# A linear-attention and SwiGLU kernel: o of the shared remainder tile by single heads, behind o of the chunks

## The chip, the core and the metric

The kernel runs on one core of one Trainium2 chip. Its engines work side by side, each in the order of its own queue: TensorE (PE, matrix products, with a queue of weight loads shown as PEld), VectorE (DVE), ScalarE (ACT), GpSimd (POOL), and SyncE (SP), which issues transfers. TensorE writes into PSUM, eight banks of 128 partitions by 512 float32; VectorE and ScalarE read them. The metric is the device time of one execution in microseconds.

## The reference

Linear attention without a softmax, a norm per head, then a gated feed-forward block (FFN) with a norm in front:

```python
# q, k, v: (8 batches, 8 heads, 576 rows, 64), float32
kv = np.einsum('bhsd,bhse->bhde', k, v)
out = np.einsum('bhsd,bhde->bhse', q, kv)                 # "o"
rms = np.sqrt(np.mean(out * out, axis=-1, keepdims=True) + 1e-06)
x = (out / rms * g_norm)                                  # then heads side by side: (4608, 512)
rms = np.sqrt(np.mean(x * x, axis=-1, keepdims=True) + 1e-06)
xn = x / rms * rms_g
g = xn @ w_gate                                           # 512 x 1536
silu = g * (1.0 / (1.0 + np.exp(-g)))
return silu * (xn @ w_val) @ w_out                        # 1536 x 512
```

## The kernel before

**Tiles.** Each batch has 576 rows: 4 chunks of 128 (NC = 4) and a remainder of 64 (REM). The remainders of two batches share a tile of 128 rows. So there are nine groups of 512 rows for the FFN: one per batch from its chunks, and one, group B, from the eight remainders. Heads go in pairs: j = 0 to 3 (NS = 4) numbers the pairs, and of a pair the even head lies on partitions 0 to 63 of `qT` and `kv`, the odd one on 64 to 127.

**The backbone.** The FFN of a group is 24 slots of the first product (12 gate slots and 12 val slots in turn, `mm1`, four matmuls of 128x512 each, L694) and 16 of the second (`mm2`, L729). A gate's result is read by ACT (silu, L703), a val's by DVE (product h, L712). The results of `mm1` lie in turn in the three PSUM banks of the pool mm1; those of `mm2` in the two banks of o2; the attention has the three banks of att. A bank is written again only when its last readers are done.

**Attention beside it.** While group g runs, the attention of the next batch is laid into the slots by a planner (`Placer`). It gives every operation an engine and a cost, puts it into the first slot in which its inputs are there and the engine has room left, and `emit` writes the program out slot by slot: first the slot's operations of ACT, DVE, POOL and SP, then the FFN's own matmuls, then the attention's matmuls. Each engine then works in that order. The costs only decide the order; the chip has its own times. `P.psum` also keeps count of the att banks: its list `P.tiles` has an entry per bank taken, with the operations that must be done before it is free.

**The steps of one batch** (`place_attention`, batches 2 to 7): q is transposed by DMA (`qT_dma`, L342; the remainder's rows L345); kv is computed (`kv_mm`, L281) and copied (`kv_half`, L310); then o of the chunks, `o_heads` (L375): 32 matmuls, each with one head, 64 rows of the array and 128 columns, 64 columns streamed. It writes four banks, two of o2 and two of att; even and odd heads go to different banks. For batch 2 and the odd batches 3, 5 and 7, o of the shared remainder tile follows: `o_rem` (L362), 8 matmuls over all 128 rows of the array and 64 of its columns, a pair of heads at a time (`kvs` holds zeros off its two diagonal blocks), 128 columns streamed, into one att bank. The two halves of the tile take the kv of two batches (`of`).

Of each of the five (or four) tiles, ACT makes a square (`sq_`, L410) and a copy (`outa_`, L414). POOL multiplies the square by the squared norm weights (`wsq`, L465), DVE sums square and product over each head (`red`, L473, twice a tile). A chain of small DVE steps makes the factors of both norms (L512 to L530), DVE scales the copies (`xna_`, L540 and L545), and SP issues transposes into x (`x_dma`, L603). The pool sq has three buffers: the fourth tile's square waits until the first tile's product has been summed.

Beside it, POOL issues the loads of the next batch's k and v (L200, and L196 for remainders) and casts q. During batch 2, ACT and DVE also multiply the weights by the norm gains (`fold`, L850 and L852), and POOL issues the loads of batch 3 at fixed slots (L963 to L965).

Of the kernel before, what the change touches and what calls it, by code (L numbers as in the profile page):

```python
# [10 lines left out]
FP32 = mybir.dt.float32  # L11
BF16 = mybir.dt.bfloat16
# [3 lines left out]
ACT = mybir.ActivationFunctionType  # L16
# [71 lines left out]
def kernel(  # L88
# [12 lines left out]
    nc = tc.nc  # L101
    B, H, S, D = q.shape
# [3 lines left out]
    NC = 4  # L106
# [16 lines left out]
    outa_p = pool("outa", 6)  # L123
    sq_p = pool("sq", 3)
# [7 lines left out]
    mm1_p = pool("mm1", 3, space=bass.MemoryType.PSUM)  # L132
    o2_p = pool("o2", 2, space=bass.MemoryType.PSUM)
    att_p = pool("att", 3, space=bass.MemoryType.PSUM)
# [115 lines left out]
    class Att:  # L250
# [103 lines left out]

        def o_rem(self):

            self.o[NC] = o = att_p.tile([128, H, D], FP32, name="att")
            of = (kvs[2], kvs[1]) if self.b == 2 else (kvs[0], kvs[1])
            for j in range(NS):
                for n in range(2):  # L360
                    at = slice(n * REM, (n + 1) * REM)
                    nc.tensor.matmul(  # L362
                        o[at, 2 * j : 2 * j + 2, :], lhsT=self.qTj[:, j, NC, at], rhs=of[n][:, j, :, :],
                        start=True, stop=True, skip_group_check=True,
                    )

        def o_heads(self):

            for n, (pool_, name) in enumerate(((o2_p, "o2"), (o2_p, "o2"), (att_p, "att"), (att_p, "att"))):
                self.o["main", n] = pool_.tile([128, 2, H // 2, D], FP32, name=name)  # L370
            for c in range(NC):
                for j in range(NS):
                    for half in range(2):
                        rows = slice(half * D, (half + 1) * D)
                        nc.tensor.matmul(  # L375
                            self.o["main", c // 2 * 2 + half][:, c % 2, j, :], lhsT=self.qTj[rows, j, c, :],
                            rhs=self.kv[rows, j, half, :], start=True, stop=True, skip_group_check=True,
                        )

        def part(self, t, n):  # L380

            if n >= NC:
                return t[:, n]
            return t[:, n // 2 * 2 : n // 2 * 2 + 2, n % 2 : H : 2]
# [232 lines left out]
    def place_attention(P, b, casts=(), at=0, chain_at=0):  # L617
        a, start = Att(b), at + 2
        V, A = nc.vector, nc.scalar
        N1 = range(a.chunks)  # L620
        P.floor = max(P.floor, at)
        load = P.put("SP", 0.0, a.qT_dma, casts[:1] if b == 2 else casts)
        qt = [("DMA", load[1] + QT_SLOTS)]
        p = P.psum(1.2, lambda: a.kv_mm(ALL), casts)
        kv = [P.reads(P.put("DVE", 0.4, lambda h=h: a.kv_half(h), [p])) for h in range(2)]
        outs, reds = {}, []
        main = P.psum(0.73, a.o_heads, kv + qt, 2)
        for c in N1:
            p = P.psum(0.3, a.o_rem, kv + qt) if c >= NC else main
            s = P.put("ACT", 0.6, lambda c=c: a.sq_(c), [p])  # L630
            outs[c] = P.put("ACT", 0.6, lambda c=c: a.outa_(c), [p])
            if c >= 2:
                P.tiles[-1 if c >= NC else c - 4] += [s, outs[c]]
            assert outs[c][1] < start + 2 * NF, (b, outs)
            w = P.put("POOL", 1.2, lambda c=c: a.wsq(c, nc.gpsimd), [s])
            reds.append(P.put("DVE", 0.68, lambda c=c: a.red(c, 0), [s]))
            reds.append(P.put("DVE", 0.68, lambda c=c: a.red(c, 1), [w]))
        prev = reds
        for n in range(0, 13, 4):
            prev = [P.put("DVE", 0.8, lambda n=n: [f() for f in a.chain(0, a.chunks)[n : n + 4]], prev, chain_at)]  # L640
        xn = [P.put("DVE", 0.68, lambda c=c: a.xna_(c, V), prev + [outs[c]]) for c in N1]
        put = [P.put("SP", 0.0, lambda c=c: a.x_dma(*c), [xn[c[1] - 1]]) for c in ((0, 2), (2, 4), (4, 5))[: a.chunks - 2]]
        return put[2 if b == B - 1 else 1][1] + X_SLOTS
# [211 lines left out]
    a = Att(0)  # L855
# [15 lines left out]
    for half in range(2):  # L871
        rows = slice(half * D, (half + 1) * D)
# [3 lines left out]
    for i, j in enumerate(P1):  # L876
        a.kv_pairs_out(kvb, i, j)
    V.tensor_scalar(
        out=gain, in0=gall[:, 0:NS], scalar1=gcol, scalar2=float(d_model) ** 0.5, op0=OP.mult, op1=OP.mult
# [29 lines left out]
    half = MAIN // 2  # L909
# [50 lines left out]
    P = Placer(slots, 3)  # L960
    casts = ()
    for b in range(1, B):
        if b == 2:  # L963
            for n, f in enumerate(loads_kv(b + 1)):
                P.at("POOL", 0.85, f, starts[1] + 11 + n)  # L965
        if b == 1:
            end = place_second(P, 10)
        else:
            s0 = starts[b - 1]
            end = place_attention(P, b, casts, s0 - 2, s0 + 2 * NF - 4)  # L970
        if os.environ.get("PLACER"):
            print("batch", b, "to", end, "wanted at", starts[b], "casts", casts)
        else:
            assert end < starts[b] + (b == 1), (b, end, starts)
        if b == 1:
            for n, at in ((0, 6), (1, 24), (2, 30), (3, 40)):
                for j in range(NS):
                    for w, eng, cost in ((wg, "DVE", 0.09), (wv, "ACT", 0.13)):
                        f = P.put(eng, cost * FB[n], lambda w=w, n=n, j=j, e=eng: fold(w[n], j, e), at=starts[1] + at + j)
                        assert f[1] < starts[2] + (2 * FB0[n] if n == 3 else 0), f  # L980
            casts = place_casts(P, 2, starts[1] - 9)
        elif b + 1 < B:
            P.put("SP", 0.0, lambda b=b: load_q(b + 1), at=starts[b - 1] + 6 * (b == 2))
            casts = place_casts(P, b + 1, starts[b - 1] + 18)
            for f in loads_kv(b + 1) if b > 2 else ():
                P.put("POOL", 0.85, f, at=starts[b - 1] + 14)
# [38 lines left out]
```

## Time and profile before

| | |
|---|---|
| runs | 321.53, 321.7, 322.65 us (median 321.7) |
| the profiled execution | 321.76 us, its span 320.0 us |
| TensorE, granted clock | 1.0 |
| `o_heads`, L375, 6 batches | 192 matmuls, 190 ns each by the profile |
| `o_rem`, L362, 4 batches | 32 matmuls, 219 ns each |
| square and copy, L410 and L414 | 28 of each, 584 to 615 ns |
| product on POOL, L465 | 28, 1154 ns |
| sums on DVE, L473 | 56, 678 ns |

Start and length in a timeline are microseconds from the span's start. The instructions of an engine overlap a little, matmuls most of all: the profile's 379 ns of a 128x512 matmul are a latency, and in the timeline such matmuls start 0.216 us apart, a group of four every 0.864. In the groups' shapes, "64*128" is the part of the array in use (rows by columns), "64x64" the streamed operand. A bracket behind a line is the idle time of its engine before it, and who ended it.

### The profile page before, as it was taken

What the parts mean: (1) busy time and instruction counts of PE and PEld (TensorE: products, weight loads), DVE (VectorE), ACT (ScalarE), POOL (GpSimd) and SP (SyncE); (2) the same over time, 40 slices, a digit from 0 to 9 for tenths busy, and PEclk for the clock granted to TensorE, in tenths of its full rate; (3) what the DMA queues carried; (4) which work ended last, traced back from release to release, by engine and by line L of the source; (5) the groups of instructions that cost most, each with busy time, mean ns of one, the idle gap of its engine ahead of it and who ended that gap; (6) DMA issues with size and microseconds to landing.
All of it is one profiled execution on the core that took longest, in us unless ns stands there. A gap on an engine that the chain in (4) does not pass through costs nothing.

```text
span 320.0 us, 5497 instructions
## 1 busy us (share of the span) xinstructions
PE 312.8 (98%) x2122; PEld 157.7 (49%) x2122; DVE 169.2 (53%) x381; ACT 138.0 (43%) x254; POOL 85.2 (27%) x105
## 2 busy tenths in 40 slices
PE   8799999999999999999999999999999999999995
PEld 3578865444444444444544444444444444444443
DVE  4565536589749651955186717571778043203410
ACT  1465454596667314632383228322842233223321
POOL 8653430077017400830075007500510000000000
PEclk9999999999999999999999999999999999999999
DMA  8999999999761974498349875964000600040002
GB/s 210 221 203 199 195 231 205 228 209 135 153 197 53 166 155 137 131 166 153 121 128 133 148 153 145 153 127 137 11 3 10 183 21 2 15 107 12 0 33 98
DMA packets 79253, 40.69 MB, mean 127 GB/s; under 512 B 42872, under 2 KB 74748, under 8 KB 79228
## 3 DMA queue, kind: packets, MB, share of 16 engines
q0 software_dynamic: 31200, 14.22, 35.1%
q1 hardware_dynamic: 46544, 25.14, 32.2%
q10 hardware_dynamic: 1484, 0.99, 1.0%
q8 instruction: 16, 0.26, 0.3%
q14 instruction: 9, 0.07, 0.1%
HBM read 37.78 MB, written 9.44 MB: 148 GB/s over the span
## 4 chain that ended last, share of the span: by engine, by line
PE 91%; DMA 8%; issue 0%; DVE 0%; ACT 0%; POOLq 0%
PE mm L694 57%; PE o L729 27%; DMA wv<-in_moe_w_val_dram 5%; DMA remv<-in_v_dram 2%; PE att L281 2%; PE mm L729 2%; PE o L375 1%; PE att L375 0%; PE att L362 0%; PE mm L756 0%; PE o L756 0%; PE att L571 0%; PE att L327 0%; PE att L423 0%; PE att L350 0%
## 5 line engine op out<-in xcount | busy, mean ns | idle before, releaser
L712 DVE TENSOR_TENSOR h<-silu,mm 128x512 bf16<-128x512 bf16 (+1 forms) x120 | 75.5, 631 | 86.9 <-PE mm L694 77.0
L703 ACT ACTIVATE silu<-mm 128x512 bf16<-128x512 f32 (+1 forms) x120 | 66.4, 556 | 86.4 <-PE mm L694 75.3
L694 PE MATMUL mm<-x,wv 128*128 128x512 bf16 (+1 forms) x432 | 99.9, 356 | 0.2 <-DMA wv<-in_moe_w_val_dram 0.2
L694 PE MATMUL mm<-x,wg 128*128 128x512 bf16 (+1 forms) x420 | 97.9, 358 | 0.0
L729 PE MATMUL o<-wo,h 128*128 128x512 bf16 x396 | 90.1, 379 | 0.0
L694 PEld LDWEIGHTS <-wv 128*128 128x128 bf16 x480 | 46.2, 98 | 45.7 <-DMA wv<-in_moe_w_val_dram 0.5
L694 PEld LDWEIGHTS <-wg 128*128 128x128 bf16 x468 | 45.1, 98 | 45.7 <-DMA wg<-in_moe_w_gate_dram 0.2
L465 POOL TENSOR_TENSOR sq<-sq,g 128x512 bf16<-128x512 bf16 x28 | 32.0, 1154 | 129.0 <-ACT sq L410 129.0
L729 PEld LDWEIGHTS <-h 128*128 128x128 bf16 x420 | 40.3, 98 | 46.5
L745 ACT COPY osb<-o 128x512 f32<-128x512 f32 x33 | 19.3, 587 | 69.1 <-PE o L729 69.1
L473 DVE TENSOR_REDUCE st<-sq 128x8 f32<-128x512 bf16 x56 | 35.9, 678 | 0.2
L310 DVE CAST kvs<-att 64x256 bf16<-64x256 f32 x14 | 5.9, 422 | 31.9 <-PE att L281 31.7
L540 DVE TENSOR_TENSOR xna<-outa,al 128x512 bf16<-128x512 bf16 x24 | 15.0, 683 | 0.0
L694 PE MATMUL mm<-xr,wg 128*128 128x512 bf16 x48 | 12.3, 379 | 0.0
L694 PE MATMUL mm<-xr,wv 128*128 128x512 bf16 x48 | 12.3, 379 | 0.0
L216 POOL CAST main_q<-stg 128x1024 bf16<-128x1024 f32 (+1 forms) x12 | 11.4, 996 | 1.1 <-DMA stg<-in_q_dram 1.1
L245 PE MATMUL mm<-idle 128*128 128x512 bf16 x27 | 9.0, 505 | 1.2 <-DVE idle L138 1.2
L410 ACT ACTIVATE sq<-att 128x512 bf16<-128x512 f32 x16 | 9.8, 615 | 0.0
L414 ACT CAST outa<-att 128x512 bf16<-128x512 f32 x16 | 9.6, 600 | 0.0
L850 ACT ACTIVATE wv<-wv,gain 128x384 bf16<-128x384 bf16 x16 | 9.0, 608 | 0.4 <-PE mm L694 0.4
L200 POOL DMA_DIRECT2D vc<-in_v_dram x9 | 7.8, 872 | 1.1 <-PE mm L694 1.1
L729 PE MATMUL mm<-wo,h 128*128 128x512 bf16 x24 | 7.8, 379 | 0.0
(132 smaller groups left out, 175.1 us busy)
## 6 DMA issues: line engine op xcount, KB each, us to landing
out_dram<-osb SPq DMA_DIRECT2D x31, 256.0 KB, 2.5
stg<-in_q_dram SPq DMA_DIRECT2D x6, 1024.0 KB, 7.5
vc<-in_v_dram POOLq DMA_DIRECT2D x7, 512.0 KB, 8.2
kc<-in_k_dram POOLq DMA_DIRECT2D x7, 512.0 KB, 6.2
wg<-in_moe_w_gate_dram POOLq DMA_DIRECT2D x4, 384.0 KB, 14.9
wv<-in_moe_w_val_dram POOLq DMA_DIRECT2D x4, 384.0 KB, 16.3
wo<-in_moe_w_out_dram POOLq DMA_DIRECT2D x4, 384.0 KB, 14.7
out_dram<-osb SPq DMA_DIRECT2D x9, 128.0 KB, 2.3
```

The costliest lines, as they stand in the source:

```text
L216: return copy(out=mains[b, t][:, cs[0] : cs[1], h0:h1, :], in_=staged[b, t].rearrange("p h (c d) -> p c h d", c=NC)[:, cs[0] : cs[1], h0:h ...
L245: nc.tensor.matmul(ps, lhsT=idle[:, :128], rhs=idle[:, : ps.shape[-1]], start=True, stop=True, skip_group_check=True)
L410: nc.scalar.activation(out=self.sq[c][:, 0], in_=self.o_of(c), func=ACT.Square)
L414: nc.scalar.copy(out=self.outa[c], in_=self.o_of(c))
L465: eng.tensor_tensor(out=self.sq[c][:, 1], in0=self.sq[c][:, 0], in1=g2, op=OP.mult)
L473: nc.vector.reduce_sum(out=self.part(self.st[:, which], c), in_=of, axis=AX.X)
L540: return eng.tensor_tensor(out=self.part(self.xna, c), in0=self.outa[c].rearrange("p (c h) d -> p c h d", c=2), in1=self.part(self.al, c). ...
L694: nc.tensor.matmul(ps[:, : c1 - c0], lhsT=w[n][:, s, jj * 128 : (jj + 1) * 128], rhs=x_of(g, s, c0, c1), start=s == 0, stop=s == NS - 1)
L703: nc.scalar.activation(out=sis[g, j][:, c0:c1], in_=ps, func=ACT.Silu)
L712: nc.vector.tensor_tensor(out=hs[g, j][:, c0:c1], in0=sis[g, j][:, c0:c1], in1=v_ps, op=OP.mult)
L729: nc.tensor.matmul(ps, lhsT=hs[g, j][:, t * 128 : (t + 1) * 128], rhs=wo[j // OB][:, j % OB, :], start=j == 0, stop=j == NF - 1)
L745: (eng.copy if eng is nc.scalar else eng.tensor_copy)(out=o, in_=ps)
```

## The change

`o_rem` no longer has a place of its own in the plan: `o_heads` calls it at its end, so its matmuls stand right behind those of the chunks. It works by single heads: 16 matmuls, each with 64 rows of the array (the head's half of the pair) and 64 of its columns (the half of the tile), 64 columns streamed. Even heads go to an att bank, odd heads to the next bank of the FFN's pool mm1. ACT then makes squares and copies in halves, odd heads first, each half over four heads (`sq_rem`, `outa_rem`; 128x256), into the same `sq` and `outa` tiles as before. The planner takes three att banks for the whole step, and handles the remainder tile first and the chunks behind it (before, it came last).

```diff
         def o_rem(self):
-            self.o[NC] = o = att_p.tile([128, H, D], FP32, name="att")
             of = (kvs[2], kvs[1]) if self.b == 2 else (kvs[0], kvs[1])
+            self.o[NC] = [
+                pool_.tile([128, H // 2, D], FP32, name=name) for pool_, name in ((att_p, "att"), (mm1_p, "mm1"))
+            ]
             for j in range(NS):
                 for n in range(2):
                     at = slice(n * REM, (n + 1) * REM)
-                    nc.tensor.matmul(
-                        o[at, 2 * j : 2 * j + 2, :], lhsT=self.qTj[:, j, NC, at], rhs=of[n][:, j, :, :],
-                        start=True, stop=True, skip_group_check=True,
-                    )
+                    for half in range(2):
+                        rows = slice(half * D, (half + 1) * D)
+                        nc.tensor.matmul(
+                            self.o[NC][half][at, j, :], lhsT=self.qTj[rows, j, NC, at],
+                            rhs=of[n][rows, j, half, :], start=True, stop=True, skip_group_check=True,
+                        )
+
+        def sq_rem(self, half):
+            if NC not in self.sq:
+                self.sq[NC] = sq_p.tile([128, 2, H, D], BF16, name="sq")
+            nc.scalar.activation(out=self.sq[NC][:, 0, half:H:2, :], in_=self.o[NC][half], func=ACT.Square)
+
+        def outa_rem(self, half):
+            if NC not in self.outa:
+                self.outa[NC] = outa_p.tile([128, H, D], BF16, name="outa")
+            nc.scalar.copy(out=self.outa[NC][:, half:H:2, :], in_=self.o[NC][half])
...
         def o_heads(self):
...
+            if self.chunks > NC:
+                self.o_rem()
...
     def place_attention(P, b, casts=(), at=0, chain_at=0):
...
-        main = P.psum(0.73, a.o_heads, kv + qt, 2)
-        for c in N1:
-            p = P.psum(0.3, a.o_rem, kv + qt) if c >= NC else main
-            s = P.put("ACT", 0.6, lambda c=c: a.sq_(c), [p])
-            outs[c] = P.put("ACT", 0.6, lambda c=c: a.outa_(c), [p])
-            if c >= 2:
-                P.tiles[-1 if c >= NC else c - 4] += [s, outs[c]]
+        rem = a.chunks - NC
+        main = P.psum(0.73 + 0.25 * rem, a.o_heads, kv + qt, 2 + rem)
+        for c in (*N1[NC:], *N1[:NC]):
+            if c == NC:
+                for n in (1, 0):
+                    s = P.put("ACT", 0.38, lambda n=n: a.sq_rem(n), [main])
+                    outs[c] = P.put("ACT", 0.38, lambda n=n: a.outa_rem(n), [main])
+                P.tiles[-1] += [s, outs[c]]
+            else:
+                s = P.put("ACT", 0.6, lambda c=c: a.sq_(c), [main])
+                outs[c] = P.put("ACT", 0.6, lambda c=c: a.outa_(c), [main])
+                if c >= 2:
+                    P.tiles[c - NC - rem] += [s, outs[c]]
```

In the built program, the order of the engines around batch 2 becomes, with the FFN's groups behind o_rem called G1 (gate), V1 (val), G2, V2 and so on:

| engine | before | after |
|---|---|---|
| PE | o_heads, gate, val, o_rem, gate ... | o_heads, o_rem, G1, V1, G2 ... |
| ACT | sq 0, silu, fold, copy 0, sq 1, silu, copy 1 ... | sq and copy of the odd half, silu G1, fold, sq and copy of the even half, silu G2, sq 0, copy 0, silu G3 ... |
| POOL | product 0, k load, product 1, k remainder, v load, v remainder, products 2, 3, remainder | product of the remainder, k load, k remainder, product 0, v load, v remainder, products 1, 2, 3 |
| DVE | one or two sums between two h | h V1, two sums, h V2, two sums, h V3 ... |

In batches 3, 5 and 7 POOL has its five products in a row, before and after. In batch 2's group, SP issues the remainder's transpose (`x_dma`, third part) one store later.

## The prediction

> **What bounds the kernel now.** I read the page first (busy shares, chain), then PE's timeline around the changed instructions, then ACT, POOL and DVE in the same stretch.
>
> ```profile
> PE 312.8 (98%) x2122; PEld 157.7 (49%) x2122; DVE 169.2 (53%) x381; ACT 138.0 (43%) x254; POOL 85.2 (27%) x105
> PE 91%; DMA 8%; issue 0%; DVE 0%; ACT 0%; POOLq 0%
> ```
>
> TensorE (PE) is busy 98% of the span and is 91% of the chain of waits. Once the loads of the start are over, every microsecond that PE spends or waits is one of the total, and what other engines do is free until PE waits for them. The timeline of PE around batch 2's attention (start, length, line, count):
>
> ```profile
> 60.99 0.82 PE L281 MATMUL att<-vc,kc 128*64 128x64 bf16 x40
> ...
> 63.48 1.03 PE L694 MATMUL mm<-x,wv 128*128 128x512 bf16 x4
> 64.44 0.41 PE L375 MATMUL o<-kvs,qTs 64*128 64x64 bf16 x16
> 64.68 0.40 PE L375 MATMUL att<-kvs,qTs 64*128 64x64 bf16 x16
> 65.01 1.04 PE L694 MATMUL mm<-x,wg 128*128 128x512 bf16 x4
> 65.89 1.03 PE L694 MATMUL mm<-x,wv 128*128 128x512 bf16 x4
> 66.84 0.41 PE L362 MATMUL att<-kvs,qTs 128*64 128x128 bf16 x8
> 67.19 1.04 PE L694 MATMUL mm<-x,wg 128*128 128x512 bf16 x4
> ```
> ```profile
> 47.67 0.61 PE L350 MATMUL att<-kvs,qTs 128*128 128x128 bf16 x8
> ```
>
> FFN groups of four follow each other every 0.864 us elsewhere. The group at 65.89 should free PE at 66.75; o_rem (L362) starts at 66.84, so changing the array's split costs 0.09. Its 8 matmuls of 219 ns in 0.41 are (0.41 - 0.219)/7 = 27 ns apart and end their turn at 67.06; the next group starts at 67.19, so changing back costs 0.13. In all PE gives o_rem 67.19 - 66.75 = 0.44 us. Pitches for later: alone, a 128-column matmul takes (0.61 - 0.219)/7 = 56 ns (L350), so 28 ns for 64 columns; two column halves side by side (L281) (0.82 - 0.196)/39 = 16 ns each; two row halves (L375) (0.41 - 0.19)/15 = 15 ns each. Two tiles of the array run at once; four at once are nowhere in this trace.
>
> ACT, POOL and DVE in the same stretch, and one form of ACT's list:
>
> ```profile
> 65.25 0.58 ACT L410 ACTIVATE sq<-o 128x512 bf16<-128x512 f32 x1
> 66.15 0.60 ACT L703 ACTIVATE silu<-mm 128x512 bf16<-128x512 f32 x1 [0.32 <-PE mm L694]
> 66.64 0.60 ACT L850 ACTIVATE wv<-wv,gain 128x384 bf16<-128x384 bf16 x1
> ```
> ```profile
> 65.97 1.15 POOL L465 TENSOR_TENSOR sq<-sq,g 128x512 bf16<-128x512 bf16 x1 [21.15 <-ACT sq L410]
> 67.07 0.95 POOL L200 DMA_DIRECT2D kc<-in_k_dram  x1
> 68.31 1.15 POOL L465 TENSOR_TENSOR sq<-sq,g 128x512 bf16<-128x512 bf16 x1 [0.28 <-ACT sq L410]
> 69.41 0.73 POOL L196 DMA_DIRECT2D kc<-in_k_dram  x1
> ```
> ```profile
> 67.62 1.31 DVE L473 TENSOR_REDUCE st<-sq 128x8 f32<-128x512 bf16 x2
> 69.20 0.69 DVE L712 TENSOR_TENSOR h<-silu,mm 128x512 bf16<-128x512 bf16 x1 [0.26 <-PE mm L694]
> ```
> ```profile
> L703 ACT ACTIVATE silu<-mm 128x256 bf16<-128x256 f32 x24 | 8.9, 386 | 9.8 <-PE mm L694 6.8 <-DVE h L712 1.8 <-PE mm L722 0.9
> ```
>
> POOL issues batch 3's k between two products of batch 2, and DVE has only 0.26 us to spare per pair of FFN groups: two reductions and one h are 3 x 0.60 = 1.80 us of a pair of 2 x 0.864 = 1.73. That margin matters below.
>
> **The change, part by part.**
>
> *PE.* Four batches (2, 3, 5, 7) lose the separate o_rem: -4 x 0.44 = -1.76 us. Each gets 16 matmuls of 64 columns behind o_heads, in its way out of the row split: one switch more, from row halves to quadrants (not in the trace; the nearest rows cost 0.09 to 0.13, so 0.10; bounds 0, if it needs no emptying, and 0.13), 0.02 for a first round that starts cold (the FFN group after a switch lasts 0.88, not 0.864), and the rounds. If four quadrants run at once, 16 x 28/4 = 0.11; if only two, 16 x 16 = 0.26; if none, 16 x 28 = 0.45. The two kinds of pairs already reach half of 28, by rows and by columns, with a new weight load per matmul; quadrants combine the two, so I take 0.11. Cost 0.23 each, 0.92 in all; bounds 4 x 0.11 and 4 x 0.60. PE's own sum: -0.84 us (-1.3 to +0.6).
>
> A rule of the Trainium skill speaks against this: TensorE: Matmul & The Clock Gate, section "Wait — 56ns, not 53.3ns?", says that starts never come closer than about 25 ns, however few the columns. By it the 16 would take 0.40 and the parts of PE would come to 4 x (0.52 - 0.44) = +0.3 us. L375's 15 ns contradict it.
>
> *The bank lent by the FFN.* mm1 has three banks in turn. The odd heads take the next one; it is wanted again by the third FFN group afterwards, 2 x 0.864 = 1.73 us after o_rem. ACT reads that half first, two reads of some 0.28 each (386 ns less the 0.1 by which neighbours overlap). In batch 2 they end at 66.0 by the replay below, for a group due at 66.98; in batch 3 at about 95.0 for 95.7. Cover 0.7 to 1.0 us: nothing. The FFN groups between them use their own banks at the old distance plus o_rem: nothing. The o2 and att banks are freed a slot or two later; o2 is wanted by the second FFN product some 16 groups on: nothing. ACT works 4 x 0.28 for 2 x 0.47, 0.2 us more of an engine at 43%: nothing on its own.
>
> *The transposed q remainder* is now needed with o_heads. It is issued on SP at 58.0 and 78.5 for o_heads at 64.4 and 93.2, and lands 3.8 us after issue: nothing.
>
> *The order behind it, batch 2.* The remainder's square comes first, but in two halves with a gate's silu and a weight fold between (ACT's order after). POOL's order after is product of the remainder, k load, k remainder load, product of chunk 0; before, a product came ahead of the k load and another behind it. Replay from the rows, with o_heads at its old 64.44 and FFN groups G1 (gate), V1 (val), G2 ... behind o_rem: G1 starts 65.01 + 0.23 = 65.24, G2 66.98, V2 67.85, V3 69.58, G5 72.17. G1's silu runs 1.07 after its start (66.31), then the fold (66.81), then the even half's square (67.31, ending 67.70). POOL follows 0.14 later, as after the sq at 65.25: product 67.83 to 68.98; the k issues take 0.92 and 0.71; product of chunk 0 from 70.58 to 71.73. DVE: remainder's second reduction 69.03, V2's h 69.62, chunk 0's first reduction 70.22, done 70.82. Its second waits for POOL until 71.78; V3's h stands behind it, 72.38 to 73.06. V3's bank is the one that G5 takes at 72.17: PE waits until 73.11, 0.94 us. Then DVE is behind, and at 1.80 against 1.73 it doesn't catch up while reductions last: 3 pairs x 0.07 = 0.21. Stall +1.15 us. The same replay of the order before gives no wait, and h, reductions and products within 0.1 us of the trace. Lower bound 0 (the wait shrinks one for one with any time gained ahead of it), upper 1.6 (an allowance; rows of the same issues differ by 0.05).
>
> *Batches 3, 5 and 7* have no load among their products (POOL's list has five products in a row). Replayed, the tightest bank is free 0.14 us (batch 3) and 0.34 us (5, 7) ahead, against 0.45 and 0.5 before: no wait. If that cover is gone, each pair costs 0.07 and more.
>
> *SP*: one remainder transpose moves behind a store; its data is wanted by the remainder group, over 100 us later: nothing.
>
> Sum: -0.84 + 1.15 = +0.3 us on the span of 320.0. The profiled execution took 321.76, 1.76 around the span, and the median of the runs is 321.7: **322.0 us**.
>
> **The rivals.**
>
> A (forecast): quadrants overlap and PE waits once in batch 2. 322.0.
>
> B: the wait isn't there; the gain stays. For: the trace has PE waiting for no bank in any steady stretch. Against: the replay's wait is 0.94 us, more than its errors. 321.7 - 0.84 = 320.9; with a free switch 320.4.
>
> C, the other side: quadrants don't overlap, each matmul waits for the weight load and stream of the one before. Place: the 16 at the end of o_heads. Price 0.10 + 0.02 + 0.45 = 0.57 against 0.44, so +0.13 each; from a pitch above 20 ns it costs more than it saves. 4 x 0.13 + 1.15 = +1.7: 323.4. For: no row shows quadrants. Against: both kinds of halves overlap.
>
> The 25 ns of that page of the Trainium skill fall here: by them +0.3 + 1.15, 323.1. The pitches of 15 and 16 ns leave it little.
>
> D: only two at a time, 16 ns each: 0.38 for 0.44, -0.06 each: -0.2 + 1.15 = +0.9: 322.6.
>
> E: the thin cover of batches 3, 5 and 7 goes too, and each waits as batch 2 does, if half as long: +0.3 + 3 x 0.6 = +2.1: 323.8 and beyond. For: 0.14 us of cover. Against: no load stands between their products.
>
> That the change isn't what it says is excluded: the built order has the 16 matmuls right behind o_heads four times.
>
> **How the numbers follow.** A 0.48, B 0.20, C 0.12, D 0.11, E 0.09. Half a per cent (1.6 us), about what a measurement of this kernel can tell from no change, lies at 320.1 and 323.3. Slower: C and E, 0.21. Faster: only scatter around B's low end, 0.05. Within: 0.74. The range runs from B's low end, 320.3, to C with 0.5 more of stall, 323.9; A's own is 321.4 to 322.6.
>
> **What would show it.** Pitch and count of the 64*64 rows (four starts in about 30 ns, 0.23 us more between o_heads and the next group): the PE part. A gap of 0.9 us on PE some eight FFN groups after batch 2's o_rem, with DVE's reduction waiting for POOL just before: the stall. No such gap: B. Gaps in batches 3, 5 or 7, or a PE wait for ACT two groups after o_rem: the prediction is wrong.

## The result, and the profile after

The changed kernel takes 322.94 us (median of 20 runs, 321.92 to 323.98), the kernel before beside it 321.84 us (20 runs, 321.46 to 322.82): a ratio of 1.0024, 95% interval 1.0013 to 1.0035. That is within the half per cent around no change. The profiled execution of the changed kernel took 323.14 us, its span 321.4.

Three stretches of its trace matter. First PE's timeline around batch 2's o (start, length, line, count; matmuls that start together have a line each; of G1's four matmuls one record is missing):

```profile
65.45 0.41 PE L389 MATMUL o<-kvs,qTs 64*128 64x64 bf16 x16
65.69 0.40 PE L389 MATMUL att<-kvs,qTs 64*128 64x64 bf16 x16
66.02 0.21 PE L366 MATMUL att<-kvs,qTs 64*64 64x64 bf16 x1
66.03 0.21 PE L366 MATMUL mm<-kvs,qTs 64*64 64x64 bf16 x1
66.03 0.21 PE L366 MATMUL att<-kvs,qTs 64*64 64x64 bf16 x1
66.03 0.21 PE L366 MATMUL mm<-kvs,qTs 64*64 64x64 bf16 x1
...
66.15 0.19 PE L366 MATMUL mm<-kvs,qTs 64*64 64x64 bf16 x1
66.27 1.04 PE L716 MATMUL mm<-x,wg 128*128 128x512 bf16 x3
```

Four quadrants start within 10 ns, and all 16 within 0.13 us. From the start of o of the chunks to G1 it is 66.27 - 65.45 = 0.82 us; without o_rem it was 65.01 - 64.44 = 0.57. So o_rem now costs 0.25 us of PE where it cost 0.44, in each of the four batches: -0.76 us in all.

Second, the stall. PE's, ACT's, POOL's and DVE's timelines, with the idle time before an instruction and who ended it in the bracket:

```profile
72.33 1.03 PE L716 MATMUL mm<-x,wv 128*128 128x512 bf16 x4
74.20 1.02 PE L716 MATMUL mm<-x,wg 128*128 128x512 bf16 x4 [0.84 <-DVE h L734]
```
```profile
67.90 0.61 ACT L872 ACTIVATE wv<-wv,gain 128x384 bf16<-128x384 bf16 x1
68.41 0.37 ACT L374 ACTIVATE sq<-att 128x256 bf16<-128x256 f32 x1
```
```profile
68.92 1.15 POOL L481 TENSOR_TENSOR sq<-sq,g 128x512 bf16<-128x512 bf16 x1 [24.27 <-ACT sq L374]
70.02 0.95 POOL L200 DMA_DIRECT2D kc<-in_k_dram  x1
70.97 0.69 POOL L196 DMA_DIRECT2D kc<-in_k_dram  x1
71.66 1.17 POOL L481 TENSOR_TENSOR sq<-sq,g 128x512 bf16<-128x512 bf16 x1
```
```profile
71.30 0.68 DVE L489 TENSOR_REDUCE st<-sq 128x8 f32<-128x512 bf16 x1
72.86 0.69 DVE L489 TENSOR_REDUCE st<-sq 128x8 f32<-128x512 bf16 x1 [0.88 <-POOL sq L481]
73.47 0.68 DVE L734 TENSOR_TENSOR h<-silu,mm 128x512 bf16<-128x512 bf16 x1
```

G5 was due at 72.33 + 0.864 = 73.19 and starts at 74.20: 1.0 us. The chain can be read upwards: PE waits for V3's h (73.47), which stands behind DVE's second sum of chunk 0 (72.86), which waited 0.88 us for POOL's product (71.66), which stands behind two issues of loads and the remainder's product (68.92), which waited for ACT's square of the even half (68.41), which stands behind a fold.

Third, what that delay does later. The first step of DVE's factor chain before the change, then DVE's list and PE's weight loads after it, where the first product ends:

```profile
77.00 0.18 DVE L512 TENSOR_SCALAR u<-st 128x40 f32<-128x40 f32 x1
```
```profile
79.41 0.35 DVE L528 TENSOR_SCALAR u<-st 128x40 f32<-128x40 f32 x1
...
82.91 0.68 DVE L734 TENSOR_TENSOR h<-silu,mm 128x512 bf16<-128x512 bf16 x1
```
```profile
81.10 2.04 PEld L751 LDWEIGHTS <-h 128*128 128x128 bf16 x10
83.64 1.41 PEld L751 LDWEIGHTS <-h 128*128 128x128 bf16 x8 [0.50 <-DVE h L734]
```

DVE's factor chain starts at 79.41 (77.00 before), so the last h of the group comes at 82.91 and its use on PE at 83.64: its matmul follows the one before by 0.384 us where the pitch is 0.216, a second wait of 0.17 us. Two things make it. Against PE's start on the second product (79.28 before, 81.10 after) the chain begins 0.59 us later than before, which uses up the 0.6 by which that h was early before (it ended at 81.01, its matmul started at 81.66). And the chain's first step, L528, takes 0.35 us for 0.18, beside a cast of POOL that runs up to 79.7: these 0.17 are what PE then waits. In the three further executions of this order of POOL (two of the experiments below, and the changed kernel with 24 idle matmuls) the step loses 0.17 to 0.18 and PE waits 0.17 to 0.18 as well; no run changes that step alone. PE's timeline has no other gap up to group 2's first FFN group, which starts, before and after the change, at:

```profile
90.50 1.03 PE L694 MATMUL mm<-x,wg 128*128 128x512 bf16 x4
```
```profile
92.50 1.03 PE L716 MATMUL mm<-x,wg 128*128 128x512 bf16 x4
```

From batch 2's o of the chunks to that group it was 90.50 - 64.44 = 26.06 us before and is 92.50 - 65.45 = 27.05: +0.99, which is -0.19 for o_rem, +1.0 and +0.17 for the waits. Batches 3, 5 and 7 have no gap, and each takes 0.19 to 0.21 us less. From batch 2's o to the end of the program it is 255.55 us before and 255.92 after: +0.37.

The rest of the difference is not behind the change in time at all. Up to about 62 us both programs have the same instructions, yet in this execution batch 2's kv came at 62.00 and in the one before at 60.99. Stretches of the start in after's and then in before's profile (busy time and matmuls, then the granted clock, DMA share, GB/s):

```profile
11.00:12.00 1.00, 1.00 (x15) 0.66 1.34 203
12.00:14.00 2.00, 2.00 (x16) 0.50 1.24 228
```
```profile
12.00:14.00 2.00, 2.00 (x27) 1.00 1.23 234
```

In the one the clock falls to 0.5 for some 3 us, in the other not. The executions of both kernels split by it: those with a mean clock up to 0.995 and those near 1.0. (Of the kernel before, this comparison has the times alone; they split at 322.2, as they do wherever its clocks are on record.) Without the drop the medians are 321.70 before and 322.02 after, with it 322.65 and 323.03: +0.32 and +0.38. The two medians above differ by 1.1 because 14 of 20 executions of the changed kernel had the drop, and 7 of 20 of the other. Whether the change has a part in that is a question for the experiments.

### The profile page after: what moved, and what is told of

It is laid out like the page before. It is cut to its first block, busy times and chain, and to the rows that moved or that the text cites. A ratio compares the mean times of both kernels' runs of the same rounds, so it can differ in the third digit from the quotient of the medians.

```text
span 321.4 us, 5541 instructions
## 1 busy us (share of the span) xinstructions
PE 310.9 (97%) x2132; PEld 158.5 (49%) x2154; DVE 168.7 (53%) x381; ACT 138.7 (43%) x262; POOL 85.2 (27%) x105
## 4 chain that ended last, share of the span: by engine, by line
PE 95%; DMA 3%; issue 1%; DVE 0%; ACT 0%; POOL 0%; DVEq 0%; POOLq 0%
PE mm L716 58%; PE o L751 26%; DMA vc<-in_v_dram 3%; PE att L281 2%; PE mm L751 2%; PE mm L297 1%; PE o L389 1%; PE att L587 1%; PE att L389 0%; PE mm L778 0%; PE o L778 0%; PE mm L744 0%; PE o L439 0%; PE att L316 0%; PE mm L245 0%
## 5 line engine op out<-in xcount | busy, mean ns | idle before, releaser
L751 PE MATMUL o<-wo,h 128*128 128x512 bf16 x382 | 87.9, 379 | 1.1 <-issue 0.6
L245 PE MATMUL mm<-idle 128*128 128x512 bf16 x26 | 7.6, 453 | 1.3 <-DVE idle L138 1.2
L426 ACT ACTIVATE sq<-att 128x512 bf16<-128x512 f32 x12 | 7.6, 633 | 0.0
L426 ACT ACTIVATE sq<-o 128x512 bf16<-128x512 f32 x12 | 7.3, 611 | 0.0
```

Of the source, the lines that this page charges most:

```text
L426: nc.scalar.activation(out=self.sq[c][:, 0], in_=self.o_of(c), func=ACT.Square)
L751: nc.tensor.matmul(ps, lhsT=hs[g, j][:, t * 128 : (t + 1) * 128], rhs=wo[j // OB][:, j % OB, :], start=j == 0, stop=j == NF - 1)
```

## The experiments

**Loads behind the products.** If the two k issues between POOL's products cause the stall, moving all four issues of batch 3's loads behind the five products removes it.

```diff
-            for n, f in enumerate(loads_kv(b + 1)):
-                P.at("POOL", 0.85, f, starts[1] + 11 + n)
+            for n in range(4):
+                P.at("POOL", 0.85, lambda: None, starts[1] + 11 + n)
+            for f in loads_kv(b + 1):
+                P.at("POOL", 0.0, f, starts[1] + 19)
```

> The changed kernel, with batch 3's four loads of k and v issued by POOL behind the five products of batch 2 (none between them); the order of every other engine is that of the changed kernel. Theory (the two k issues hold POOL's product of chunk 0, DVE's sum waits for it, V3's h behind it keeps the bank that G5 wants): the 1.0 us gap of TensorE ahead of G5 goes to 0.1 or less, at most 0.15 in all at the next pairs, and the time is 0.9 us below the changed kernel's: about 321.1 in executions with an undisturbed start and 322.1 in those whose clock drops at the start, ratio to before about 0.998. Rival 1 (the halves on ACT and the lent bank make the gap): the gap stays at 1.0 us and the time at 322.0 to 323.1. Rival 2 (the loads later make the next batch late): the gap goes, but TensorE waits for k or v at batch 3's kv, around 91 us, and gives it back.

Measured: 323.12 us (12 runs, one with the drop; ratio 1.0040, interval 1.0026 to 1.0054). That is 1.0 us above the changed kernel without the drop, where the theory had 0.9 below it. But the gap ahead of G5 is gone (72.27 for a due 72.23). The time is given back later, in waits that neither the theory nor a rival had; DVE, POOL and PE of this run:

```profile
77.48 1.37 DVE L528 TENSOR_SCALAR u<-st 128x40 f32<-128x40 f32 x1
78.89 0.40 DVE L529 RECIPROCAL r<-u 128x40 f32<-128x40 f32 x1
79.32 0.52 DVE L530 SCALAR_TENSOR_TENSOR t<-st,r 128x40 f32<-128x40 f32 x1
```
```profile
77.73 2.04 POOL L216 CAST main_q<-stg 128x1024 bf16<-128x1024 f32 x2
79.70 0.63 POOL L223 CAST remq<-rstg 128x512 bf16<-128x512 f32 x1
```
```profile
83.05 7.51 PE L751 MATMUL o<-wo,h 128*128 128x512 bf16 x33 [1.18 <-DVE h L734]
...
92.72 1.02 PE L716 MATMUL mm<-x,wg 128*128 128x512 bf16 x4 [0.86 <-DMA x<-xna]
```

POOL's casts, late by the moved issues, now lie over the factor chain; two steps of it that last 0.18 and 0.20 us otherwise take 1.37 and 0.52, the group's last h is late (PE's bracket says 1.18), then the x transposes (0.86). Three groups of the first product come 0.06 late each besides, since DVE needs 1.78 us for two sums and an h where a pair of groups takes 1.73. From o of the chunks to group 2 it takes 28.23 us for 27.05. So the issues cause the wait at G5, and their new place is worse.

**Four issues ahead.** The opposite: all four issues between the first two products.

```diff
+            for n in range(4):
+                P.at("POOL", 0.85, lambda: None, starts[1] + 11 + n)
             for n, f in enumerate(loads_kv(b + 1)):
-                P.at("POOL", 0.85, f, starts[1] + 11 + n)
+                P.at("POOL", 0.0, f, starts[1] + 11 + n // 2)
```

> The changed kernel, with all four issues of batch 3's loads between the product of the remainder and that of chunk 0 (two more than in the changed kernel); the order of every other engine is kept. Theory: the gap ahead of G5 grows by the two issues, 0.93 + 0.70 = 1.6 us, from 1.0 to 2.6 us, and the span by 1.6 us. Rival 1 (ACT and the bank): the gap stays at 1.0 us.

Measured, one execution: 323.51 us, no clock drop, so it compares with 322.02. DVE's sum now waits 2.45 us for POOL:

```profile
73.31 0.69 DVE L489 TENSOR_REDUCE st<-sq 128x8 f32<-128x512 bf16 x1 [2.45 <-POOL sq L481]
```
```profile
72.27 1.02 PE L716 MATMUL mm<-x,wg 128*128 128x512 bf16 x4
74.64 1.02 PE L716 MATMUL mm<-x,wv 128*128 128x512 bf16 x4 [1.34 <-DVE h L734]
```

G5 waits 0.2 and V5, due at 73.13, 1.5; o of the chunks in batch 2 to group 2 takes 28.46 us, +1.4 for a forecast +1.6. Rival 1 is excluded. But only 0.7 of the 1.4 is waited here; the rest comes later, 0.06 at each of three groups and 0.7 for the group's last h, where the changed kernel waits 0.17. And it is V5 that waits for V3's h: the three mm1 banks are not taken strictly in turn.

**Even half first.** ScalarE reads the attention bank first and the lent bank second.

```diff
-                for n in (1, 0):
+                for n in (0, 1):
```

> The changed kernel, with ACT reading the even half (the att bank) first and the odd half (the FFN's bank) second, so that in batch 2 the lent bank is kept until behind a fold, about 2 us longer. Theory: the cover of 1.0 us ahead of G2 is gone and TensorE waits there about 1.0 us for ACT; POOL's product starts no later than before, since both halves are read at the same times in the other order, so G5 then comes due 1.0 us later and no longer waits (0 to 0.1): the gap moves, the span stays within 0.2 us. Batches 3, 5 and 7, without a fold, wait 0. Rival (the lent bank costs by itself, beside the stall of G5): both gaps stand, span 1.0 us longer.

Measured, one execution: 322.95 us, with the clock drop (so beside 323.03). G2 is late by 0.05 and V2 by 0.18, G5 by 0.79; 27.06 us to group 2, as in the changed kernel. The sum was as expected, its parts were not, again because the banks are not strictly in turn. Which half is read first is worth nothing; POOL needs both.

**Quadrant by quadrant.** The 16 matmuls in another order: all four heads of one quadrant, then the next.

```diff
-            for j in range(NS):
-                for n in range(2):
-                    at = slice(n * REM, (n + 1) * REM)
-                    for half in range(2):
-                        rows = slice(half * D, (half + 1) * D)
+            for n in range(2):
+                at = slice(n * REM, (n + 1) * REM)
+                for half in range(2):
+                    rows = slice(half * D, (half + 1) * D)
+                    for j in range(NS):
```

> The changed kernel, with the 16 matmuls of o_rem in another order: four in a row in the same quadrant, then the next quadrant. Theory (the quadrants work side by side, and a matmul waits only for the one before it in its own quadrant, 28 ns): starts 28 to 30 ns apart within a quadrant, the 16 take 0.45 instead of 0.12 us, TensorE's turn for o_rem grows from 0.25 to 0.55 to 0.6 us, span +0.3 us in each of batches 3, 5, 7 (in batch 2 the wait ahead of G5 takes it up in part): +1.0 to +1.3 us. Rival (the array takes matmuls at one every few ns whatever the quadrant): starts stay 3 to 4 ns apart and nothing changes.

Measured, one execution: 322.22 us, no clock drop. PE's timeline:

```profile
64.96 0.21 PE L366 MATMUL att<-kvs,qTs 64*64 64x64 bf16 x1
64.97 0.21 PE L366 MATMUL mm<-kvs,qTs 64*64 64x64 bf16 x1
64.99 0.21 PE L366 MATMUL att<-kvs,qTs 64*64 64x64 bf16 x1
65.00 0.21 PE L366 MATMUL mm<-kvs,qTs 64*64 64x64 bf16 x1
```

In the program four matmuls into att now come first, then four into mm; the trace starts them in turn, the two row halves side by side, about 13 ns apart, and the first four of att 26 to 27 ns apart, close to the 28 of the theory. All 16 start within 0.16 us, not 0.45, because different parts of the array still overlap. From o of the chunks to G1 it is 0.85 us for 0.82. So the overlap doesn't hang on a neat order, and the finer order is worth 0.03 us a batch.

**The start.** Both kernels with 24 instead of 18 idle matmuls at the beginning, which shortens PE's wait for the first load.

```diff
-    spin(mm1_p.tile([128, MAIN], FP32, name="mm1"), 18)
+    spin(mm1_p.tile([128, MAIN], FP32, name="mm1"), 24)
```

> The changed kernel with 24 instead of 18 idle matmuls at the very start (six more at about 0.22 us fill the time in which TensorE waited 2.6 us for the first load in its profile). Theory: the higher of the two groups of executions of both kernels (0.9 to 1.0 us above the lower one) is that wait, in which the clock falls to 0.5; with it filled all executions fall into the lower group: about 322.0 us, none above 322.6. Rival: the higher group has another source in the change; then the executions still split, some at 323.0 and over.

> The kernel before with the same 24 idle matmuls. Theory: all executions in its lower group, 321.5 to 322.0 us, median about 321.7 (0.2 us more if the idle matmuls now end behind the first load where the clock came late), so the change by itself costs 0.3 to 0.4 us. Rival (the change alters how often the clock falls, and so is worth 1.1 us): the two kernels with 24 still differ by over 0.7 us.

Measured: 322.08 us changed (11 runs, 321.88 to 322.36) and 321.73 before (11 runs, 321.64 to 322.07), none with a drop, while 10 of 25 runs of the unedited kernel before beside them had it. The difference of the means is 0.35 us (95%: 0.22 to 0.48). That is what the change costs. The profiles say the same without the start: from batch 2's o to the end 255.56 us before and 255.95 after, each within 0.03 of the profile with 18.

Does the change alter how often the clock falls? Over all runs here with 18 idle matmuls, 31 of 82 executions of the kernel before had the drop, and 19 of 44 of the kernels with the change or a variant of it: 14 of 20 in the first comparison (7 of 20 beside them), 1 of 12 with the loads behind the products (5 of 17), 3 of 9 below (10 of 25), and one of the three single executions. Of the three comparisons only the first has more of it with the change. That it has nothing to do with the change is not shown.

**Both squares first.** If the stall begins with ACT's even square, which waits behind a silu and a fold, then bringing that square forward removes it and leaves the loads where they are.

```diff
-                for n in (1, 0):
-                    s = P.put("ACT", 0.38, lambda n=n: a.sq_rem(n), [main])
-                    outs[c] = P.put("ACT", 0.38, lambda n=n: a.outa_rem(n), [main])
+                for f in (lambda: a.sq_rem(1), lambda: a.sq_rem(0), lambda: a.outa_rem(1)):
+                    s = P.at("ACT", 0.38, f, main[1] + 1)
+                outs[c] = P.put("ACT", 0.38, lambda: a.outa_rem(0), [main])
```

> The changed kernel with ScalarE's four operations on the remainder in another order: both squares, then the odd copy, then the even copy (which stays where it was, behind the first silu and fold). GpSimd's product of the remainder can start about 1.75 us earlier (67.15 for 68.92 in the profile's time), its two issues of loads end by 69.9, and the product of chunk 0 then starts when ScalarE's square of chunk 0 is done (70.3 for 71.7), so that the second sum of chunk 0 waits for nothing and V3's h starts at 72.5 for 73.5. Theory (the 1.0 us ahead of G5 is a chain from ScalarE's even square over GpSimd's issues to V3's h): G5 waits under 0.1 us, and from o of the chunks in batch 2 to group 2's first FFN group it takes 26.1 to 26.2 us for 27.05; the other batches do not change; casts end before the factor chain, so nothing is given back: about 0.9 us less than the changed kernel in the same kind of start, 0.5 to 0.7 us less than the kernel before, 321.0 us with an undisturbed start. Rival: the wait moves to another group (the lent bank is given back 0.28 us later, or ScalarE's silu of G1 comes late): a gap at G2 or V2 of the same size, and no gain.

> Squares first and 24 idle matmuls together. Theory: all executions in one group, 321.0 us (0.9 to 1.0 under the changed kernel with 24, 0.6 under the kernel before with 24), a ratio of 0.997 to 0.998 to the kernel before. Rival: as the changed kernel with 24.

Measured: 321.11 us with 18 idle matmuls (9 runs; ratio 0.9979, interval 0.9967 to 0.9991; without the drop 321.05 beside 321.73) and 320.93 with 24 (5 runs, 320.87 to 321.10; 0.9964, 0.9951 to 0.9976). The run with 18, PE, ACT, then POOL:

```profile
71.37 1.03 PE L716 MATMUL mm<-x,wv 128*128 128x512 bf16 x4
72.23 1.03 PE L716 MATMUL mm<-x,wg 128*128 128x512 bf16 x4
```
```profile
65.72 0.38 ACT L374 ACTIVATE sq<-att 128x256 bf16<-128x256 f32 x1
```
```profile
66.24 1.15 POOL L481 TENSOR_TENSOR sq<-sq,g 128x512 bf16<-128x512 bf16 x1 [21.48 <-ACT sq L374]
67.34 0.96 POOL L200 DMA_DIRECT2D kc<-in_k_dram  x1
68.29 0.69 POOL L196 DMA_DIRECT2D kc<-in_k_dram  x1
69.34 1.15 POOL L481 TENSOR_TENSOR sq<-sq,g 128x512 bf16<-128x512 bf16 x1 [0.36 <-ACT sq L426]
```

POOL starts 1.75 us after o of the chunks (64.49) where it took 3.47 (65.45 to 68.92), its product of chunk 0 waits for ACT instead of for its own issues, and G5 comes on its pitch. From o of the chunks to group 2: 25.95 us, 1.1 less than the changed kernel, and 0.1 less than before. Both waits are gone; of the 0.19 us that o_rem saves here, 0.09 goes to two groups that come 0.03 and 0.06 late, at DVE's pace. From batch 2's o to the end it takes 254.82 us for 255.55 before.

**The move without the quadrants.** The same placement with 24 idle matmuls, but the remainder's o by pairs into one attention bank, with one square and one copy.

```diff
-            self.o[NC] = [
-                pool_.tile([128, H // 2, D], FP32, name=name) for pool_, name in ((att_p, "att"), (mm1_p, "mm1"))
-            ]
+            self.o[NC] = o = att_p.tile([128, H, D], FP32, name="att")
...
-                for f in (lambda: a.sq_rem(1), lambda: a.sq_rem(0), lambda: a.outa_rem(1)):
-                    s = P.at("ACT", 0.38, f, main[1] + 1)
-                outs[c] = P.put("ACT", 0.38, lambda: a.outa_rem(0), [main])
+                s = P.at("ACT", 0.6, lambda: a.sq_(NC), main[1] + 1)
+                outs[c] = P.put("ACT", 0.6, lambda: a.outa_(NC), [main])
```

> The move without the quadrants, with 24 idle matmuls: the remainder's o is right behind o of the chunks and read first, but by pairs of heads as before (8 matmuls of 128 rows into one attention bank, no bank of the FFN lent), ScalarE reads it by one square of 128x512 and one copy. GpSimd's order is then that of the kernel before, one issue between the first and the second product, so no wait at G5 by the chain theory. Theory (the quadrants by themselves save TensorE's time, 0.25 us for 0.34 a batch behind o of the chunks; half of what the old place cost comes from the switch of row groups that the new place saves): about 0.35 us more than squares first with 24, 321.3 us, and 0.4 less than the kernel before with 24; o of the chunks to the next FFN group in batch 2: 0.57 + 0.34 = 0.91 us for 0.82. Rival 1 (all comes from the place): as squares first with 24, 320.9. Rival 2 (all comes from the quadrants): as the kernel before with 24, 321.7, and 1.0 us from o of the chunks to the next FFN group.

> The kernel with both squares first and 24 idle matmuls once more, beside the pairs on the same chip: 320.9 to 321.1 us, all executions in one group.

Measured: 321.28 us by pairs (12 runs; one, 322.85, had the clock drop in spite of 24), 321.06 by quadrants (8 runs; ratio 0.9969, 0.9958 to 0.9980). The pairs in PE's timeline:

```profile
64.17 0.41 PE L389 MATMUL o<-kvs,qTs 64*128 64x64 bf16 x16
64.41 0.40 PE L389 MATMUL att<-kvs,qTs 64*128 64x64 bf16 x16
64.74 0.41 PE L362 MATMUL att<-kvs,qTs 128*64 128x128 bf16 x8
65.09 1.04 PE L716 MATMUL mm<-x,wg 128*128 128x512 bf16 x4
```

From o of the chunks to G1 it is 0.92 us, so pairs cost 0.35 here, against 0.44 in the old place and 0.25 for quadrants. Time and trace lie where the theory had them, between the two rivals. The PE time that the change saves comes about half from each: 0.09 from the place (as much as one change of the array's split cost in the old trace) and 0.10 from the quadrants. In the medians the place gives 0.45 (321.73 to 321.28, on two occasions) and the quadrants 0.2 (321.28 to 321.06). The profiles, from batch 2's o to the end, have less scatter: 255.56 us for the kernel before, 255.14 by pairs and 254.81 by quadrants, so 0.42 and 0.33. Four batches of 0.10 would be 0.4: batches 3, 5 and 7 give 0.09 to 0.10 each, batch 2 only 0.04, because of the 0.09 us lost to DVE's pace (0.03 by pairs). The 0.2 of the medians does not contradict the 0.33: without the one drop the means differ by 0.25 us (95%: 0.10 to 0.41).

## Why the prediction was right

The forecast was 322.0 us by -0.84 for PE and +1.15 for the stall, and the kernel gives 322.08 with its start undisturbed, 322.94 as the median of the runs.

- *PE's sum.* Predicted 0.23 us for each o_rem in quadrants, measured 0.25; -0.76 for -0.84. The first round is slower than the later ones, about 0.05 for 0.03 us. The choice to take four quadrants at once from two kinds of halves was right: rivals C and D are excluded by the starts. The 25 ns between starts that the Trainium skill gives (TensorE: Matmul & The Clock Gate, "Wait — 56ns, not 53.3ns?") do not hold where matmuls use different parts of the array: 16 starts in 0.13 us.
- *The stall.* Its place and chain came out as replayed, and its size to 0.07 us. Moved by the later start of this execution (1.01 us), the replay has the remainder's product at 68.84, chunk 0's at 71.59, V3's h at 73.39 and G5 at 74.12; the trace has 68.92, 71.66, 73.47 and 74.20. The replay let G1's silu begin 1.07 us after its group; behind a change of the array's split it is 1.14 (67.41 - 66.27, and already 66.15 - 65.01 in the profile before), and that shift goes down the whole chain: 1.01 us of wait for 0.94. The 3 x 0.07 us behind it did not appear as small delays of the next groups. PE waited 0.17 once, for the group's last h, and as much as L528 lost beside a cast; the replay had no such contention. DVE's pace of 1.78 us (not 1.80) for 1.73 is real, but shows on PE only in other runs, as delays of 0.03 to 0.06 a pair of groups (loads behind the products, four issues ahead, both squares first). That the total is 1.18 for 1.15 is luck in this second part. Rival B is excluded by the gap, and is what the kernel does once both squares come first.
- *The lent bank* cost nothing, as predicted, though "three banks in turn" was too strict: which bank a group takes varies, as two experiments showed. It made no difference to the forecast.
- *Batches 3, 5 and 7* wait for nothing, though the replay left batch 3 a cover of only 0.14 us; rival E is excluded.
- *The sum.* +0.3 predicted, +0.35 measured with the start filled (interval 0.22 to 0.48), +0.32 and +0.38 within each kind of start. The other 0.7 us of the measured difference of medians was not in the prediction: it is the start's clock drop, which came more often in one set of runs than in the other.

## What to carry to other kernels

When work on a busy engine is made shorter and moved, follow the helper engines' queues in their new order: here TensorE gained 0.76 us and lost 1.18, because one read of 0.38 us on ScalarE came after a silu and a fold, with GpSimd's load issues behind it. Replaying the queues from the durations of the old trace gave the wait to within 0.1 us, and also showed the mend: bring forward the one instruction that the chain begins with (320.9 to 321.1 us for 321.7), rather than move the loads, which only collided elsewhere. When differences are below a microsecond, compare executions that had the same start.

## What the hardware showed that was not expected

The start's clock. In the two profiles above, PE's wait for the first v load is 2.61 us in the one where the clock then falls and 1.48 in the other:

```profile
10.34 0.38 PE L297 MATMUL mm<-vc,main_k 128*128 128x128 bf16 x4 [2.61 <-DMA vc<-in_v_dram]
```
```profile
10.43 0.38 PE L297 MATMUL mm<-vc,main_k 128*128 128x128 bf16 x4 [1.48 <-DMA vc<-in_v_dram]
```

The 22 idle matmuls ahead of it (18, and 4 of a later step) took 6.53 us there and 7.75 here: their starts, 0.427 us apart at first and 0.216 later, change over at about 4.5 us and at about 7.0, which is taken here as the time at which the clock became full. The Trainium skill (TensorE: Matmul & The Clock Gate, "What's actually happening") says that the clock is set by activity in windows of 3.4 us that run on by themselves, whatever the kernel does. The traces agree: counted on from 4.5, a window ends at 11.3 us, 2.4 us of it idle, and the clock falls there (the 0.66 of the stretch from 11 to 12 above); counted on from 7.0, the window up to 10.4 has 1.4 us idle, and it stays full. Two of the experiments lie close to the border between the two. In both the starts change over at 5.0, so a window runs from 8.4 to 11.8. With the even half first the load came at 10.30, 1.9 us of that window were idle, and the clock fell at 11.8; with the loads behind the products it came at 10.11, 1.7 us were idle, and it did not. With 24 instead of the 18, 46 of 47 executions had no drop.

VectorE beside GpSimd's casts. In the changed kernel's profile, L528 (tensor_scalar, 128x40, 0.18 us otherwise) began at 79.41 while POOL's second cast of 128x1024 ran, and ended at 79.76, just behind the cast (about 79.7). In the run with the loads behind the products it began at 77.48, during POOL's last issue of a load, and ended at 78.85, just behind the first of the casts that followed (about 78.75); L530, with two inputs in SBUF, began at 79.32 and ended at 79.84, behind the second (79.77). L529, a reciprocal, lay wholly inside that second cast and took its usual 0.40. The Trainium skill (SBUF — State Buffer, "Who interferes with whom") says that VectorE's tensor_scalar in its two-port modes, and, beside a GpSimd instruction that reads SBUF, instructions with two inputs in SBUF, need a port pair that GpSimd holds for a whole instruction, and that others do not. These rows agree with it. In the profiles of the kernel before and of both squares first, the same tensor_scalar began within 0.01 us of POOL's third cast (128x512), lay inside it and took its usual 0.18, while the cast took 0.65 for 0.60; who had the ports first there the trace does not show.
